# Sums by accumulating transfers of GpSimd instead of VectorE additions, in a mixed Fourier and sliding-window attention kernel

## The chip, the core and the metric

The kernel runs on one core of a Trainium2 chip. The metric is the device time of one execution in microseconds (us), the lower the better. The engines are called as the profile calls them: PE is TensorE (matmuls; PEld its weight loads), DVE is VectorE, ACT is ScalarE, POOL is GpSimd, SP is SyncE, which here only issues transfers.

## What is computed

Two layers read the same `x` (2048 rows of 512) and are mixed by a gate. All is float32.

```python
a = einsum("bsd,ed->bse", x, dft_hid_re); b = einsum("bsd,ed->bse", x, dft_hid_im)
A = einsum("ts,bse->bte", dft_seq_re, a) - einsum("ts,bse->bte", dft_seq_im, b)   # Fourier mixing

q, k, v = split(x @ wqkv)                  # 32 heads of 16
s = (q @ k.T) / 4, kept where 0 <= row - column < 256
B = (softmax(s) @ v) @ wo                  # sliding-window attention

g = sigmoid((x * gate_w).sum(-1))
out = g * A + (1 - g) * B
```

## The kernel before

**Precision.** TensorE multiplies numbers of fewer bits than float32, so every operand is kept as two tiles, a rounded "high" part (a cast, on ScalarE) and a "low" part (the original minus the high part, a 128x512 subtraction). A product is three matmuls: high by high, high by low, low by high. The low parts of the sequence-transform matrices (`lo<-raw,hi`) are made by VectorE during attention and by GpSimd once the list `FIN` is filled, when the attention loop has ended (`attention_done`).

**Two streams on TensorE.** The attention loop runs over 8 groups of 4 heads times 16 row blocks of 128 (128 steps `n`, each of four quarters). In each quarter it issues a small piece of attention and then (`fill`) a number of matmuls from `dense()`, a generator that computes everything else: projections, hidden transform, then the sequence transform. So attention is spread evenly over the dense work, and the two share the engines. All other attention work is put on an agenda by quarter (`at_time(t, ...)`), and the engines keep the order in which instructions are written out.

**Attention.** `s_pair` multiplies queries by keys into PSUM (a bank pair of the pool `ps_a`, tag `st`, two of them), and VectorE adds the mask and takes the row minimum (`junk<-s,mask` with its read-out `ml`), which frees the banks. Some steps later `t_pair` computes the transposed scores with the minimum folded in, ScalarE takes the exponential (`pt<-t`), and GpSimd zeroes what lies outside the window (`AFFINE_SELECT pt<-pt`). Every fourth step comes a *visit* (32 in all): `pv` multiplies 512 rows of `pt` by the values into two PSUM banks, one for each half of the array's rows. The visit then ends in a chain, at the offsets (in quarters) of the tuple `far`:
- `o_evict`: ScalarE copies both banks to `ots`, a tile of three 512-wide slots; the second bank always goes to slot 2, the first in turn to slot 0 or 1
- `o_add`: VectorE adds slot 2 to the other
- `l_move`: SyncE moves the softmax denominators, 4 rows of 512, to a 128x16 tile (`lt<-ots`); `l_turn`: VectorE's RECIPROCAL; `l_inv` and `l_back`: to DRAM and back, spread over the rows (`ev<-l_scr`)
- `o_mul`: GpSimd multiplies (`ev<-ots,ev`); `o_out` stores to `o_scr`.

**The sequence transform.** The output has 16 row blocks `tb`; each is a sum over 16 blocks of each of two matrix halves, cosine by `a` (half 0) and sine by `b` (half 1), in two steps `j` of eight. A step is 24 pairs of matmuls, on the upper and the lower 64 rows of the array at the same time (`halves64`). The steps are grouped in threes, and a block's steps do not all follow one another: `SWITCH`, `LATE` and the list `keys` say which come when (kind `f`: both `j` in one accumulation; kind `h`: each `j` by itself). So a partial sum, already scaled by the gate `g1`, is stored in DRAM (`r_scr`) and taken up later. The first term of a block is evicted by ScalarE and stored (`store_r`). A later term fetches the partial sum into a tile `ev` (5 buffers) 42 beats ahead (`FETCH`; a beat is one step of the dense stream), VectorE computes `ps * g1 + r` in one SCALAR_TENSOR_TENSOR (`add_to`), and SyncE stores the result in another copy of `r_scr`. There are 21 such additions. The last terms of nine blocks (`c_block`) and the output projection (`wo_...`) come after attention and are the tail.

**Loads of the sequence matrices** (`raw<-cr`, `raw<-ci`, 512 KB, three buffers) are issued by GpSimd during attention and by SyncE afterwards, each when the low parts of the piece three earlier have been made.

Of the kernel before, what the change touches and what calls it, by code (L numbers as in the profile page):

```python
# [7 lines left out]
F32 = mybir.dt.float32  # L8
F32R = mybir.dt.float32r
AF = mybir.ActivationFunctionType  # L10
OP = mybir.AluOpType
# [3 lines left out]
P = 128  # L15
# [30 lines left out]
def fnet_window_mix(ctx: ExitStack, tc: tile.TileContext, xT, x, wqk, wv, wr, wi, cr, ci, wo, gw, out):  # L46
# [15 lines left out]
    m_scr = [dram.tile([2, 16, P], F32, name=f"m_scr{i}") for i in range(32)]  # L62
    l_scr = [dram.tile([HG, 512], F32, name=f"l_scr{i}") for i in range(32)]
    o_scr = [dram.tile([NG, 32, 2, HG, 512], F32, name=f"o_scr{i}") for i in range(4)]
    r_scr = [[dram.tile([P, D], F32, name=f"r_scr{i}_{c}") for c in range(16)] for i in range(3)]

    def ld(dst, src):
        mark("sp", nc.sync.dma_start(dst, src))

    def ld_pool(dst, src):  # L70
        nc.gpsimd.dma_start(dst, src)

    def f(ap):
        return ap.bitcast(F32)
# [59 lines left out]
        return hi, lo  # L134

    jobs = []
    due = []
    beats = [0]

    def after(n, fn, *args):  # L140
        due.append((beats[0] + n, lambda: fn(*args)))  # L141
# [10 lines left out]
    def split_soon(raw, on_dve=False):  # L152
        hi = st.tile([P, 1024], F32R, name="hi")
        lo = st.tile([P, 1024], F32R, name="lo")
        for c in HALVES:
            jobs.append(lambda c=c: nc.scalar.copy(hi[:, c], raw[:, c]))  # L156
            jobs.append(lambda c=c: (nc.gpsimd if FIN else nc.vector).tensor_sub(lo[:, c], raw[:, c], f(hi[:, c])))  # L157
        return hi, lo

    def job(n):  # L160
# [305 lines left out]
        nc.scalar.copy(ots[:, 0:3:2] if i % 2 == 0 else ots[:, 1:3], o)  # L466

    def o_add(i):
        nc.vector.tensor_add(OT[i], OT[i], ots[:, 2])

    LT = {}

# [15 lines left out]
    def o_mul(i):  # L488
        ot, rl = OT.pop(i), LT.pop(i)
        nc.gpsimd.tensor_mul(rl, ot, rl)  # L490
        OT[i] = rl

    def o_out(i):
        rl = OT.pop(i)
# [155 lines left out]
    def dense():  # L650
# [138 lines left out]
        order += [ab_part(0, sb, do(*AB0.get(sb, ()))) for sb in range(16)]  # L789
        groups = [order[:4], *(order[i:i + 3] for i in range(4, len(order), 3))]  # L790

        def store_r(tb, o):
            t = ev.tile([P, 512], F32, name="ev")
            nc.scalar.activation(t, o.ps, AF.Copy, scale=g1[:, tb:tb + 1])
            after(STORE, ld, r_scr[0][tb], t)

        def fetch(src):
            def load():
                r = ev.tile([P, 512], F32, name="ev")
                ld(r, src)  # L800
                return r
            return load

        def add_to(dst, tb, o):
            nc.vector.scalar_tensor_tensor(o.r, o.ps, g1[:, tb:tb + 1], o.r, op0=OP.mult, op1=OP.add)
            after(STORE, ld, dst, o.r)

        def shortly(fn):
            return lambda o: after(2, fn, o)

        def r_in(tb):
            return r_scr[2 if tb in lasts else 0][tb]

        def finish(tb):
            return shortly(lambda o: add_to(r_scr[1][tb], tb, o))

        todo_b = [*SC]

# [6 lines left out]

        def c_get(k):
            kind, half, tb, j = k
            o = outs.get((half, tb)) if kind == "f" or j else None
            if kind == "f":
                if j == 0:  # L830
                    o = outs[half, tb] = Out(shortly(lambda o: store_r(tb, o)) if half == 0 else finish(tb), 2,
                                             None if half == 0 else fetch(r_in(tb)))
            elif half == 0:
                o = (Out(shortly(lambda o: store_r(tb, o))) if j == 0 else
                     Out(shortly(lambda o: add_to(r_scr[2][tb], tb, o)), 1, fetch(r_scr[0][tb])))
            else:
                o = (Out(shortly(lambda o: add_to(r_scr[2][tb], tb, o)), 1, fetch(r_in(tb))) if j == 0 else
                     Out(finish(tb), 1, fetch(r_scr[2][tb])))
            n = slots[kind, half, j] = slots.get((kind, half, j), -1) + 1
            mid = {4: pieces.load}  # L840
            if kind == "h" and half != j:
                if n in (1, 2, 3, 4, 5):
                    mid[12] = next_b
                if n in (1, 3, 5):
                    mid[20] = next_b
            return Part(o, lambda: c_ops(pieces.get((half, tb * 2 + j)), ab if half == 0 else nxt, j), 24,
                        pre=pieces.split, mid=mid)
# [9 lines left out]
        have.add("halves")  # L857

        def load_r(tb):
            return mixed.pop(tb, None) if tb > 13 else fetch(r_in(tb))()  # L860

        def add_r(tb, ps, r):
            nc.vector.scalar_tensor_tensor(r, ps, g1[:, tb:tb + 1], r, op0=OP.mult, op1=OP.add)
# [116 lines left out]
    def r_load(i):  # L980
        k = 4 if i == R15 else i % 2 * 2
        R[i] = RT[0][:, k], RT[0][:, k + 1]
        for tb, t in zip(O[i][0], R[i]):
            with behind("sp"):
                ld(t, r_scr[2 if i == R15 else 1][tb])

    def sums(eng, s1, s2, s3, s4, a, b):
        eng.tensor_add(s1, b[:, :256], b[:, 256:])
# [144 lines left out]
    for i in range(4 * GROUPS):  # L1133
        t = 4 * (VISIT * i + VISIT + LAG) + 3
        at_time(t + 0.5, pv, i)
        far = (0.5, 2, 3, 9, 11, 16, 21, 24) if i == 4 * GROUPS - 1 else (0.5, 2, 4, 11, 15, 21, 28, 32)
        for d, fn in zip(far, (o_evict, o_add, l_move, l_turn, l_inv, l_back, o_mul, o_out)):
            at_time(t + d, fn, i)
        if i:
            at_time(t + 2, v_next, i + 2)  # L1140
            at_time(t + 12, v_spread, i + 2)
# [75 lines left out]
```

## Time and profile before

| what | value |
|---|---|
| time, median of 2 runs | 839.9 us (839.17 to 840.64) |
| profiled execution | 838.5 us, its span 836.7 us |
| TensorE matmuls busy | 813.9 us (97%) |
| VectorE busy | 541.4 us (65%), 1536 instructions |
| ScalarE busy | 430.9 us (51%) |
| GpSimd busy | 378.6 us (45%) |
| granted TensorE clock | 0.998 of full speed |
| bytes moved by DMA | 168.98 MB, mean 202 GB/s |

The profile is one execution. Its span runs from the first to the last instruction; the execution's own time is 1.8 us longer. Lines L... are lines of the kernel file, and a line can be that of a helper: `L542` is every matmul of `halves64`, `L71` every load issued by GpSimd, `L68` every transfer issued by SyncE. In a row, `out<-in` names tiles without their numbers; `x` is the count, then busy time in us, mean ns of one, and the idle time of the engine just before with the instruction that ended it.

### The profile page before, as it was taken

The page shows a single profiled execution, that of the slowest core. Times are in us where ns is not written, and L with a number is a line of the kernel's source. Part 1 is how long each engine was busy: PE and PEld are TensorE (multiplying, and loading weights), DVE is VectorE, ACT ScalarE, POOL GpSimd, SP SyncE. Part 2 cuts the span into 40 slices and gives each one's busy share as a digit, 9 for nine tenths or more (in the row PEclk, how much of TensorE's full clock was granted, in tenths as well). Part 3 has the DMA queues.
Part 4 walks back from the last instruction along what each step waited for, and adds up shares of the span by engine and source line. Part 5 has one row for each costly group of instructions (what it writes and reads, how often), then busy time and mean ns, then how long its engine had stood idle before and what let it go on. Part 6 is the DMA issues. An engine that isn't in the chain of part 4 may idle for free.

```text
span 836.7 us, 22652 instructions
## 1 busy us (share of the span) xinstructions
PE 813.9 (97%) x8706; PEld 661.6 (79%) x8706; DVE 541.4 (65%) x1536; ACT 430.9 (51%) x814; POOL 378.6 (45%) x683
## 2 busy tenths in 40 slices
PE   9999999999999998999999999999999999899998
PEld 7899877887778777888877887777777877788886
DVE  7276765566776777666766666887887546455453
ACT  6225664556555656555655666565655653323220
POOL 5002444444444435444554444564644555765440
PEclk9999999999999999999999999999999999999999
DMA  9875887668878456555666667887885657765531
GB/s 341 288 216 154 268 264 202 182 181 293 299 256 249 114 140 180 136 176 148 189 154 185 156 182 211 233 252 229 236 230 167 198 162 226 261 196 189 168 114 51
DMA packets 109355, 168.98 MB, mean 202 GB/s; under 512 B 34240, under 2 KB 43968, under 8 KB 109248
## 3 DMA queue, kind: packets, MB, share of 16 engines
q1 hardware_dynamic: 96192, 127.04, 51.0%
q0 software_dynamic: 11088, 39.33, 15.4%
q8 instruction: 68, 1.11, 0.6%
q10 hardware_dynamic: 1968, 1.18, 0.5%
q14 instruction: 39, 0.32, 0.1%
HBM read 107.74 MB, written 59.51 MB: 200 GB/s over the span
## 4 chain that ended last, share of the span: by engine, by line
PE 77%; DVE 10%; DMA 6%; issue 4%; ACT 2%; POOL 1%; SPq 0%; DVEq 0%; POOLq 0%; ACTq 0%
PE d L542 43%; PE dc L595 8%; PE o L458 8%; PE s L364 5%; PE t L1027 5%; PE t L423 4%; DVE junk L368 4%; PE d L582 3%; DMA raw<-ci 2%; DVE lo L157 1%; DMA lt<-ots 1%; DMA o_scr<-ev 1%; DMA r_scr<-ev 1%; DVE big L141 1%; PE s L294 1%
## 5 line engine op out<-in xcount | busy, mean ns | idle before, releaser
L368 DVE CUSTOM_DVE_ANT_0 junk<-s,mask 128x384 f32<-128x384 f32 (+2 forms) x512 | 272.0, 531 | 174.4 <-PE s L364 163.6
L542 PE MATMUL d<-big,hi 64*128 64x512 f32 x1920 | 345.7, 396 | 0.0
L428 POOL TENSOR_SCALAR_AFFINE_SELECT pt<-pt 128x256 f32<-128x256 f32 x256 | 122.3, 478 | 340.1 <-ACT pt L426 274.7
L426 ACT ACTIVATE pt<-t 128x768 f32<-128x768 f32 (+2 forms) x256 | 197.8, 773 | 113.3 <-PE t L423 109.6
L542 PEld LDWEIGHTS d<-big,hi 64*128 64x128 f32 x1920 | 192.3, 186 | 24.5 <-issue 0.9
L542 PE MATMUL d<-big,lo 64*128 64x512 f32 x960 | 205.4, 395 | 0.0
L542 PE MATMUL d<-hi,big 64*128 64x512 f32 x672 | 135.7, 395 | 0.0
L542 PEld LDWEIGHTS d<-big,lo 64*128 64x128 f32 x960 | 98.9, 186 | 12.4 <-issue 0.5
L364 PE MATMUL s<-ring,ring 48*128 48x384 f32 (+2 forms) x512 | 96.3, 342 | 6.7 <-DVE ml L368 6.2
L156 ACT CAST hi<-raw 128x512 fp32r<-128x512 f32 x142 | 87.1, 618 | 25.9 <-DMA raw<-ci 15.4
L432 POOL TENSOR_SCALAR_AFFINE_SELECT pt<-pt 128x256 f32<-128x256 f32 x224 | 94.6, 422 | 0.0
L595 PE MATMUL dc<-big,hi 128*128 128x512 f32 x284 | 92.1, 394 | 0.0
L157 DVE TENSOR_TENSOR lo<-raw,hi 128x512 fp32r<-128x512 f32 x110 | 85.5, 779 | 9.6 <-ACT hi L156 9.6
L423 PE MATMUL t<-ring,ring 50*128 50x384 f32 (+2 forms) x512 | 87.2, 328 | 0.8 <-DMA ring<-m_scr 0.3
L542 PEld LDWEIGHTS d<-hi,big 64*128 64x128 f32 x672 | 78.9, 186 | 6.6 <-issue 0.2
L542 PE MATMUL d<-lo,big 64*128 64x512 f32 x336 | 84.0, 394 | 0.0
L364 PEld LDWEIGHTS s<-ring,ring 48*128 48x128 f32 x512 | 53.5, 184 | 37.4 <-DVE ml L368 23.4
L458 PEld LDWEIGHTS o<-pt,vt 64*32 64x32 f32 x2816 | 53.9, 106 | 28.9 <-issue 9.2
L458 PE MATMUL o<-pt,vt 64*32 64x320 f32 (+4 forms) x2816 | 74.7, 348 | 2.1 <-DVE ml L368 1.9
L466 ACT COPY ots<-o 128x1024 f32<-128x1024 f32 x32 | 32.5, 1016 | 73.6 <-PE o L458 31.0
L157 POOL TENSOR_TENSOR lo<-raw,hi 128x512 fp32r<-128x512 f32 x32 | 43.8, 1379 | 39.6 <-ACT hi L156 39.5
L423 PEld LDWEIGHTS t<-ring,ring 50*128 50x128 f32 x512 | 50.3, 184 | 12.8 <-ACT pt L426 1.3
(124 smaller groups left out, 914.6 us busy)
## 6 DMA issues: line engine op xcount, KB each, us to landing
ring<-qk_scr SPq DMA_DIRECT2D x128, 192.0 KB
qk_scr<-home SPq DMA_DIRECT2D x32, 512.0 KB
raw<-cr POOLq DMA_DIRECT2D x32, 512.0 KB, 5.2
r_scr<-ev SPq DMA_DIRECT2D x44, 256.0 KB
raw<-ci POOLq DMA_DIRECT2D x18, 512.0 KB, 6.3
qk_scr<-home SPq DMA_DIRECT2D x32, 256.0 KB
ev<-l_scr SPq DMA_DIRECT2D x32, 256.0 KB
o_scr<-ev SPq DMA_DIRECT2D x32, 256.0 KB
```

Of the source, the lines that this page charges most:

```text
L156: jobs.append(lambda c=c: nc.scalar.copy(hi[:, c], raw[:, c]))
L157: jobs.append(lambda c=c: (nc.gpsimd if FIN else nc.vector).tensor_sub(lo[:, c], raw[:, c], f(hi[:, c])))
L364: nc.tensor.matmul(ps[:, h, :w], ring[0][r, p, j * P:j * P + P], ring[1][r, p, k0:k0 + w], start=True, stop=True)
L368: mark("dve", nc.vector.tensor_tensor_reduce(out=junk[:, :w], in0=ps[:, h, :w], in1=mask[:, WIN - w:], scale=1.0, scalar=3e38, op0=OP.add, ...
L423: nc.tensor.matmul(ps[:, h, :w], ring[1][r, p, q0:q0 + P], ring[0][r, p, q0:q0 + w], start=True, stop=True)
L426: nc.scalar.activation(pt[:, ph, :w], ps[:, :, :w], AF.Exp, scale=-1.0)
L428: nc.gpsimd.affine_select(a, a, pattern=[[0, 2], [1, P]], compare_op=OP.is_ge, fill=0.0, base=0, channel_multiplier=-1)
L432: nc.gpsimd.affine_select(a, a, pattern=[[0, 2], [-1, P]], compare_op=OP.is_gt, fill=0.0, base=0, channel_multiplier=1)
L458: nc.tensor.matmul(o[32 * j:32 * j + 32, h, a - q0:e - q0], v[r, kb % 4, 32 * j:32 * j + 32], PT[G * NB + kb][r, j, a - kb * P:e - kb * P] ...
L542: nc.tensor.matmul(o.ps, lhs[r], rhs[r], start=start, stop=end and o.left == 0, skip_group_check=True)
L595: nc.tensor.matmul(ps, w[a][:, i % 8 * 128:i % 8 * 128 + 128], ab[SC[i]][:, b], start=i == ends[0] and a + b == 0, stop=i == ends[1] and a ...
L1027: nc.tensor.matmul(ps, o[:, a, c], fin(n, b, c), start=start and c == 0 and a + b == 0, stop=c == 1 and a == 1, skip_group_check=True)
```

## The change

- **A visit's two banks.** `o_add` no longer is a VectorE instruction but a transfer issued by GpSimd, from slot 2 of `ots` into slot 0 or 1 with the option that adds to the target. `l_move` comes one quarter later (offset 5 instead of 4); in the last visit the offsets from `l_move` on are 1 or 1.5 later.
- **Partial sums.** Every term is evicted by ScalarE with the gate's factor. The first of a block is stored by SyncE as before, each later one is added to the block in DRAM by an accumulating transfer of GpSimd. The fetches, VectorE's additions and the third copy of `r_scr` are gone. The last terms of nine blocks (`c_block`) still fetch and add on VectorE.
- **Low parts.** GpSimd takes over the low parts when the last visit's `o_mul` has been written out, not at the end of the attention loop; seven of them so stay on VectorE.

TensorE's instructions and their order are the same.

```diff
+    def add_pool(dst, src):
+        nc.gpsimd.dma_start(dst, src, accum_op=OP.add)
...
     def split_soon(raw, on_dve=False):
...
-            jobs.append(lambda c=c: (nc.gpsimd if FIN else nc.vector).tensor_sub(lo[:, c], raw[:, c], f(hi[:, c])))
+            jobs.append(lambda c=c: (nc.gpsimd if done else nc.vector).tensor_sub(lo[:, c], raw[:, c], f(hi[:, c])))
...
     def o_add(i):
-        nc.vector.tensor_add(OT[i], OT[i], ots[:, 2])
+        add_pool(OT[i], ots[:, 2])
...
     def o_mul(i):
...
+        if i == 4 * GROUPS - 1:
+            done.append(True)
...
+        sent = set()
+
         def store_r(tb, o):
             t = ev.tile([P, 512], F32, name="ev")
             nc.scalar.activation(t, o.ps, AF.Copy, scale=g1[:, tb:tb + 1])
-            after(STORE, ld, r_scr[0][tb], t)
+            after(STORE, add_pool if tb in sent else ld, r_scr[0][tb], t)
+            sent.add(tb)
...
-        def add_to(dst, tb, o):
-            nc.vector.scalar_tensor_tensor(o.r, o.ps, g1[:, tb:tb + 1], o.r, op0=OP.mult, op1=OP.add)
-            after(STORE, ld, dst, o.r)
...
         def c_get(k):
             kind, half, tb, j = k
...
-            elif half == 0:
-                o = (Out(shortly(lambda o: store_r(tb, o))) if j == 0 else
-                     Out(shortly(lambda o: add_to(r_scr[2][tb], tb, o)), 1, fetch(r_scr[0][tb])))
-            else:
-                o = (Out(shortly(lambda o: add_to(r_scr[2][tb], tb, o)), 1, fetch(r_in(tb))) if j == 0 else
-                     Out(finish(tb), 1, fetch(r_scr[2][tb])))
+            o = outs.get((half, tb)) if kind == "f" and j else None
+            if o is None:
+                o = outs[half, tb] = Out(shortly(lambda o: store_r(tb, o)), 2 if kind == "f" else 1)
...
-        far = (0.5, 2, 3, 9, 11, 16, 21, 24) if i == 4 * GROUPS - 1 else (0.5, 2, 4, 11, 15, 21, 28, 32)
+        far = (0.5, 2, 4.5, 10, 12, 17, 22, 25) if i == 4 * GROUPS - 1 else (0.5, 2, 5, 11, 15, 21, 28, 32)
         for d, fn in zip(far, (o_evict, o_add, l_move, l_turn, l_inv, l_back, o_mul, o_out)):
```

Three places show what moves. First VectorE at the visit that the profile has at 558.7 us, in the stage of second terms. ISA rows are the mask-and-reduce pairs, `big<-stage` and `lo<-raw,hi` are low parts. Before:

```order
L141 TENSOR_TENSOR big<-stage,big 128x512
L368 ISA junk,ml<-s,mask 128x384
L368 ISA ml 128x1
L368 ISA junk,ml<-s,mask 128x384
L368 ISA ml 128x1
L469 TENSOR_TENSOR ots<-ots 128x512
L805 SCALAR_TENSOR_TENSOR ev<-d,g_309,ev 128x512
L157 TENSOR_TENSOR lo<-raw,hi 128x512
L368 ISA junk,ml<-s,mask 128x384
```

And with the change, at the same place on VectorE:

```order
L145 TENSOR_TENSOR big<-stage,big 128x512
L372 ISA junk,ml<-s,mask 128x384
L372 ISA ml 128x1
L372 ISA junk,ml<-s,mask 128x384
L372 ISA ml 128x1
L161 TENSOR_TENSOR lo<-raw,hi 128x512
L372 ISA junk,ml<-s,mask 128x384
```

The visit's addition and the addition of a partial sum are gone from between the reductions and the next low part.

Second, GpSimd at the same visit. `AFFINE_SELECT` rows are the window masks on `pt`, `stage` and `raw` are loads. Before:

```order
L71 DMA stage<-ab_scr_11_129 128x512
L71 DMA raw<-ci 128x1024
L428 AFFINE_SELECT pt<-pt 128x2x128
L432 AFFINE_SELECT pt<-pt 128x2x128
L428 AFFINE_SELECT pt<-pt 128x2x128
L432 AFFINE_SELECT pt<-pt 128x2x128
L428 AFFINE_SELECT pt<-pt 128x2x128
L432 AFFINE_SELECT pt<-pt 128x2x128
```

And with the change, on GpSimd:

```order
L71 DMA stage<-ab_scr_11_129 128x512
L71 DMA raw<-ci 128x1024
L432 AFFINE_SELECT pt<-pt 128x2x128
L436 AFFINE_SELECT pt<-pt 128x2x128
L74 DMA ots<-ots 128x512
L432 AFFINE_SELECT pt<-pt 128x2x128
L436 AFFINE_SELECT pt<-pt 128x2x128
L74 DMA r_scr_13_215<-ev 128x512
```

The accumulating transfers of the visit and of a partial sum now stand between the masks, behind the mask of the first exponential after the visit's eviction.

Third, SyncE at the same visit, from the load of the values to the next ring load. Before:

```order
L68 DMA vr<-v_scr_112 128x4x64
L68 DMA lt<-ots 128x1x16
L68 DMA ev<-l_scr_189 128x1x512
L68 DMA r_scr_13_247<-ev 128x512
L68 DMA r_scr_15_249<-ev 128x512
L68 DMA ev<-r_scr_0_202 128x512
L68 DMA r_scr_14_248<-ev 128x512
L68 DMA ring_285<-qk_scr_3_1_91 48x2x512
```

And with the change, on SyncE:

```order
L68 DMA vr<-v_scr_112 128x4x64
L68 DMA ev<-l_scr_189 128x1x512
L68 DMA lt<-ots 128x1x16
L68 DMA ring_269<-qk_scr_3_1_91 48x2x512
L68 DMA ring_270<-qk_scr_3_1_107 48x2x512
```

The move of the denominators has gone behind the visit before's `ev<-l_scr`, and the stores and fetches of partial sums behind it are gone.

More of the change, by code (lines that the diff above doesn't have):

```diff
@@ L64, in fnet_window_mix @@
     o_scr = [dram.tile([NG, 32, 2, HG, 512], F32, name=f"o_scr{i}") for i in range(4)]
-    r_scr = [[dram.tile([P, D], F32, name=f"r_scr{i}_{c}") for c in range(16)] for i in range(3)]
+    r_scr = [[dram.tile([P, D], F32, name=f"r_scr{i}_{c}") for c in range(16)] for i in range(2)]
     def ld(dst, src):
@@ L136, in fnet_window_mix @@
     jobs = []
+    done = []
     due = []
@@ L802, in fetch @@
             return load
-        def add_to(dst, tb, o):
-            nc.vector.scalar_tensor_tensor(o.r, o.ps, g1[:, tb:tb + 1], o.r, op0=OP.mult, op1=OP.add)
-            after(STORE, ld, dst, o.r)
         def shortly(fn):
             return lambda o: after(2, fn, o)
[L811 to L815, printed above, removed]
         todo_b = [*SC]
@@ L827, in c_get @@
             kind, half, tb, j = k
[L828 to L832, printed above, removed]
-            elif half == 0:
-                o = (Out(shortly(lambda o: store_r(tb, o))) if j == 0 else
-                     Out(shortly(lambda o: add_to(r_scr[2][tb], tb, o)), 1, fetch(r_scr[0][tb])))
-            else:
-                o = (Out(shortly(lambda o: add_to(r_scr[2][tb], tb, o)), 1, fetch(r_in(tb))) if j == 0 else
-                     Out(finish(tb), 1, fetch(r_scr[2][tb])))
+            o = outs.get((half, tb)) if kind == "f" and j else None
+            if o is None:
+                o = outs[half, tb] = Out(shortly(lambda o: store_r(tb, o)), 2 if kind == "f" else 1)
             n = slots[kind, half, j] = slots.get((kind, half, j), -1) + 1
@@ L859, in load_r @@
         def load_r(tb):
-            return mixed.pop(tb, None) if tb > 13 else fetch(r_in(tb))()
+            return mixed.pop(tb, None) if tb > 13 else fetch(r_scr[0][tb])()
         def add_r(tb, ps, r):
@@ L984, in r_load @@
             with behind("sp"):
-                ld(t, r_scr[2 if i == R15 else 1][tb])
+                ld(t, r_scr[int(i != R15 and tb >= 16 - LATE)][tb])
     def sums(eng, s1, s2, s3, s4, a, b):
```

## The prediction

> **What bounds the kernel now.** I read the page's first lines, then the same busy times by stage, then what TensorE waited for.
>
> ```profile
> span 836.7 us, 22652 instructions
> PE 813.9 (97%) x8706; PEld 661.6 (79%) x8706; DVE 541.4 (65%) x1536; ACT 430.9 (51%) x814; POOL 378.6 (45%) x683
> ```
>
> TensorE (PE) is busy for all but 22.8 us of the span, and the change leaves its instructions and their order alone. So whatever is won has to come out of those 22.8 us, and any loss is a new wait of TensorE.
>
> ```profile
> core 0: us, PE busy (x) PEld busy (x) DVE busy (x) ACT busy (x) POOL busy (x), PEclk, DMA share, GB/s
> 100.00:340.00 240.00, 232.00 (x2858) 184.46 (x2856) 162.44 (x524) 137.34 (x264) 107.31 (x223) 1.00 0.71 214
> 340.00:520.00 180.00, 179.64 (x2296) 145.17 (x2294) 120.49 (x382) 107.66 (x195) 84.37 (x175) 1.00 0.64 172
> 520.00:640.00 120.00, 115.08 (x1389) 89.47 (x1395) 96.70 (x276) 69.31 (x126) 64.83 (x124) 1.00 0.79 229
> 640.00:700.00 60.00, 60.00 (x700) 47.88 (x683) 34.51 (x66) 33.27 (x62) 28.59 (x53) 1.00 0.63 187
> 700.00:836.00 136.00, 128.89 (x710) 108.32 (x708) 63.70 (x106) 33.29 (x68) 67.75 (x62) 0.99 0.52 169
> ```
>
> Column one is the stage, two its length, three TensorE's busy time. TensorE idles 8.0 us in 100 to 340 (projections and the hidden transform), 0.4 in 340 to 520 (first terms of the sequence transform), 4.9 in 520 to 640 (where second terms are added to partial sums), nothing in 640 to 700, 7.1 in the tail. Who is waited for:
>
> ```profile
> PE s L364 <- DVE ml L368: 6.2, 13, 0.9
> PE s L384 <- DVE ml L368: 3.7, 7, 1.0
> PE o L458 <- DVE ml L368: 1.9, 3, 1.4
> PE t L1027 <- ACT ex L141: 3.8, 1, 3.8
> ```
>
> Columns: total, times, longest. 11.8 us in 23 waits go to VectorE (DVE), whose mask-and-reduce pair (L368) frees the PSUM bank that TensorE needs next. One wait of 3.8 lies in the tail. One of the 23, in the stage that the change lightens most:
>
> ```profile
> 560.71 0.69 DVE L469 TENSOR_TENSOR ots<-ots 128x512 f32<-128x512 f32 x1
> 561.32 0.75 DVE L805 SCALAR_TENSOR_TENSOR ev<-d,g,ev 128x512 f32<-128x512 f32 x1
> 561.98 0.77 DVE L157 TENSOR_TENSOR lo<-raw,hi 128x512 fp32r<-128x512 f32 x1
> 562.66 0.55 DVE L368 CUSTOM_DVE_ANT_0 junk<-s,mask 128x384 f32<-128x384 f32 x1
> 563.87 0.44 PE L364 MATMUL s<-ring,ring 48*128 48x384 f32 x2 [0.73 <-DVE ml L368]
> ```
>
> Three 128x512 instructions stand ahead of the reductions, and TensorE waits 0.73 us. The first two are exactly the two kinds that the change removes.
>
> **The change part by part.** The prices:
>
> ```profile
> L469 DVE TENSOR_TENSOR ots<-ots 128x512 f32<-128x512 f32 x32 | 22.0, 686 | 4.8 <-ACT ots L466 4.8
> L805 DVE SCALAR_TENSOR_TENSOR ev<-d,g,ev 128x512 f32<-128x512 f32 x21 | 15.5, 739 | 12.4 <-PE d L542 12.4
> L794 ACT ACTIVATE ev<-d,g 128x512 f32<-128x512 f32 x16 | 11.0, 688 | 0.6 <-PE d L542 0.6
> L157 DVE TENSOR_TENSOR lo<-raw,hi 128x512 fp32r<-128x512 f32 x110 | 85.5, 779 | 9.6 <-ACT hi L156 9.6
> L157 POOL TENSOR_TENSOR lo<-raw,hi 128x512 fp32r<-128x512 f32 x32 | 43.8, 1379 | 39.6 <-ACT hi L156 39.5
> L71 POOL DMA_DIRECT2D raw<-cr x32 | 18.1, 567 | 0.8 <-issue 0.8
> 520.00:640.00 120.00, 10.29 (x14) 1.00 0.79 229
> ```
>
> The last row counts VectorE's instructions on `ev` in 520 to 640: 14 of the 21 partial-sum additions, 10.3 us.
>
> *VectorE, 520 to 640.* Gone are these 14 and six visit additions (6 x 0.686 = 4.1), together 14.4 of 96.7 us. What stays, 82.3 in 120 us, is 69% busy; the stage 340 to 520 runs at 120.5/180 = 67% with 0.4 us of idle TensorE. I take the same for this stage, about 0.5 instead of 4.9: **-4.4** (bounds -4.9 and 0, the latter if the waits only move).
>
> *VectorE, 100 to 340.* Here 12 additions go (8.2 us of 162.4). The stage is already at 68%, so density is not what hurts; single pile-ups are. Of its 13 waits of TensorE that carry VectorE's name, from the first to the last
>
> ```profile
> 114.83 0.44 PE L364 MATMUL s<-ring,ring 48*128 48x384 f32 x2 [0.26 <-DVE ml L368]
> 334.56 0.44 PE L364 MATMUL s<-ring,ring 48*128 48x384 f32 x2 [0.45 <-DVE ml L368]
> ```
>
> five have a visit addition in the VectorE work just ahead (3.0 us together), and an addition can give back no more than its 0.69: **-2.8** (bounds -3.0 and 0). The others sit behind low parts and gate products, which stay.
>
> *ScalarE.* It evicts the 21 second terms instead: 21 x 0.688 = 14.4 us, 14 of them in 520 to 640, where it goes from 69.3 to 78.9 us of 120 (66%). The cover is the spare bank of the `t` products; the one row of a wait there is small:
>
> ```profile
> PEld t L423 <- ACT pt L426: 1.3, 3, 0.5
> PEld o L458 <- POOL pt L432: 4.3, 6, 1.8
> ```
>
> **+0.5** (bounds 0 and 4.4, what the same instructions cost on VectorE). In exchange these evictions wait for no fetched partial sum.
>
> *GpSimd (POOL).* 32 + 21 = 53 issues more at the price of a load's, 0.567: 30.1 us. Seven low parts leave (7 x 1.38 = 9.7), so it ends near 399 us, 48%. Behind each issue stand the mask selects of `pt`, which a visit's products need four steps later; six times TensorE's weight loads already wait there. Each issue can push one of those by 0.57, 3.4 in all; I take **+0.5** (bounds 0 and 3.4). Here the Trainium skill speaks against the change: in "SBUF — State Buffer", section "SBUF: two separate sides", it warns that DMAs issued from GpSimd starve while VectorE runs an instruction that takes both shared ports, since GpSimd cannot write their descriptors. By that rule I would take the upper bound, 3.4. The trace does not show it: the 32 issues above mean 0.567 us next to a VectorE that is two thirds busy, so I keep 0.5.
>
> *The new wait.* SyncE's move of the denominators (`lt<-ots`) now waits for the accumulating transfer, and VectorE's reciprocal (L478) keeps its place. The visit of the example above, the tightest visit outside the end, and the nearest durations:
>
> ```profile
> 562.15 0.85 POOL L432 TENSOR_SCALAR_AFFINE_SELECT pt<-pt 128x256 f32<-128x256 f32 x1
> 571.93 0.25 DVE L478 RECIPROCAL lt<-lt 128x16 f32<-128x16 f32 x1
> 169.26 0.40 POOL L432 TENSOR_SCALAR_AFFINE_SELECT pt<-pt 128x256 f32<-128x256 f32 x1
> 177.10 0.25 DVE L478 RECIPROCAL lt<-lt 128x16 f32<-128x16 f32 x1
> DMA to landing us min/median/max: 2.9/5.8/8.1
> 690.05 0.56 SPq L68 DMA_DIRECT2D lt<-ots  x1
> 695.48 0.25 DVE L478 RECIPROCAL lt<-lt 128x16 f32<-128x16 f32 x1 [0.55 <-DMA lt<-ots]
> DVE junk L368 <- PE s L364: 163.6, 137, 7.1
> ```
>
> GpSimd can issue the addition after the select, at 563.0, and the reciprocal stood at 571.9: 8.9 us of room (7.4 in the tight visit). No accumulating transfer is in the trace. The nearest is a load of the same 256 KB on the same queue: the row of 2.9/5.8/8.1 is that of the 20 `stage<-ab_scr` loads. The small move behind it took 5.4 in the crowded tail (690.05 to 695.48) and, as the fastest transfer of that row, hardly under 2.9. So the chain is 5.8 at best from two times 2.9, 13.5 at worst, and I take 5.8 + 3.0 = 8.8, the median load and a move near its fast end, since outside the tail no reciprocal waited. That fits the room of an ordinary visit by a hair and misses the tight one by 1.4 us. VectorE itself waits 163.6/137 = 1.2 us for TensorE at a typical pair, which absorbs most of it. Behind a late reciprocal stand the next reductions and low parts, and TensorE behind those. I take **+2** (bounds 0 and 32, below). The skill's fit in "DMA: Bandwidth & Descriptors", section "Anatomy of one DMA — SWDGE (gpsimd) path", of 2.0 us plus bytes over 436 GB/s is an estimate of 2.6 us for 256 KB, with which this +2 would be 0; the loads here took 5.8, and I go by them.
>
> *SyncE* loses 42 transfers (21 stores, 21 fetches) and gains a block of some 7 us per visit at `lt<-ots`; behind it stand ring loads that the old trace issued no earlier than at 572 in this visit, so I cost it at nothing. Without that cover a late ring load would stop TensorE, up to the size of the late chain itself.
>
> *The tail.* The 3.8 us wait is a chain:
>
> ```profile
> 700.71 2.55 POOL L157 TENSOR_TENSOR lo<-raw,hi 128x512 fp32r<-128x512 f32 x2 [0.45 <-ACT hi L156]
> 703.29 0.35 SPq L68 DMA_DIRECT2D raw<-ci  x1
> 713.18 0.62 ACT L156 CAST hi<-raw 128x512 fp32r<-128x512 f32 x1 [5.43 <-DMA raw<-ci]
> ```
>
> GpSimd's two low parts end at 703.26 and free the buffer, the next load goes out, lands 9.8 us later, and ScalarE is stuck behind it. On VectorE the two take 2 x 0.78, 1.0 us less. Against that, the last visit's `lt<-ots` (690.05) waits for its accumulation: eviction ended at 685.8, an issue of 0.6 and 5.8 of landing make 692.2, and the first of these loads stands behind it on SyncE. So 2 us later there, 1 earlier here: **+0.5** (bounds -5, if wait and the slow products after it vanish, and +6, if each of three reciprocals holds the low parts by 2).
>
> **Sum:** -4.4 - 2.8 + 0.5 + 0.5 + 2 + 0.5 = -3.7. The profiled execution took 838.5 (span plus 1.8), so 834.8; the median of the two timed runs, 839.9, lies 1.4 above it: **836**.
>
> **The rivals.**
> 1. *Slower: the reciprocal waits in every visit.* If the transfer takes 5.8 and the move 5.4, the chain is 11.2, 2.3 over the room and 1.1 over room plus slack. 29 visits before the tail then cost 32 us instead of 2: **866**. It decides from a chain of 8.9 + 1.2 = 10.1 us on. For it: that an accumulation must also read its target. Against: the fast end of the rows.
> 2. *More is won.* VectorE's relief takes away all waits of 100 to 640 but those of the quiet density, 12.9 us, and the new wait costs nothing: 838.5 - 12.9 + 1.4 = **827**. Against: eight of 13 waits in 100 to 340 have no removed instruction ahead.
> 3. *No change.* Evictions on ScalarE and issues on GpSimd delay `pt` as much as VectorE is relieved, so the change of engine buys nothing: 838.5 - 3.7 + 4.4 + 0.5 + 1.4 = **841**.
>
> **How the numbers follow.** The forecast, 831 to 842 by its smaller bounds, gets 0.50, rival 1 0.17, rival 2 0.13, rival 3 0.20. The range 825 to 862 holds the forecast, rivals 2 and 3, and the milder half of rival 1 (a chain near 10.5). Within 2% (about what a measurement of this kernel tells from no change) is 823.1 to 856.7: 0.83; slower 0.13, most of rival 1; faster 0.04, beyond rival 2.
>
> **What would show it.** In the new profile: VectorE near 510 us; TensorE idle under 1 us in the stage of second terms; reciprocals waiting for `lt<-ots` in few visits outside the end; accumulating rows on GpSimd of about 0.57 us landing near 6. I am wrong if reciprocals wait in most visits, if `t` products start to wait for ScalarE, or if the issue rows on GpSimd are several times as long.

## The result: 891.4 us, six per cent slower, and the profile after

The changed kernel takes 891.44 us (median of 2 runs, 888.26 to 894.63) against 839.9: a ratio of 1.061, 95% interval 1.045 to 1.078. The forecast was 836, range 825 to 862. Rival 1, the reciprocal that waits for the denominators, is what happened, in 19 visits and at a higher price than its 866.

The page's first lines, of the profiled execution after:

```profile
span 892.9 us, 22556 instructions
PE 828.5 (93%) x8706; PEld 670.4 (75%) x8706; DVE 513.2 (57%) x1490; ACT 442.2 (50%) x835; POOL 407.9 (46%) x729
```

VectorE is relieved as planned (513 us for 541), and it didn't help. The span is 56.2 us longer. TensorE idles 64.4 us (892.9 less 828.5) instead of 22.8, and the same 8706 matmuls are busy for 14.6 us longer. By stage (columns as in the prediction; the boundaries lie where TensorE reaches the work it had reached at 340, 520, 640 and 700):

```profile
100.00:363.00 263.00, 238.14 (x2860) 187.92 (x2858) 156.78 (x516) 137.48 (x265) 114.61 (x235) 0.97 0.73 208
363.00:546.00 183.00, 180.01 (x2292) 145.44 (x2290) 115.03 (x369) 107.58 (x195) 91.35 (x184) 0.99 0.68 180
546.00:680.00 134.00, 119.62 (x1380) 93.07 (x1384) 85.72 (x256) 76.68 (x138) 80.21 (x144) 0.95 0.78 188
680.00:750.00 70.00, 62.25 (x705) 48.74 (x689) 21.55 (x53) 37.09 (x69) 33.57 (x59) 0.93 0.61 144
750.00:893.00 143.00, 130.71 (x715) 109.64 (x713) 70.21 (x117) 33.30 (x68) 62.64 (x59) 0.98 0.52 167
```

The stages are 23, 3, 14, 10 and 6 us longer than before. The least is lost in the stage of first terms. Who waits (total, times, longest), of the list of waits:

```profile
DVE lt L482 <- DMA lt<-ots: 65.2, 19, 10.5
PE s L368 <- DVE ml L372: 27.0, 14, 8.5
PE o L462 <- POOL pt L432: 6.0, 1, 6.0
PE t L1018 <- ACT ex L145: 5.9, 1, 5.9
SPq L68 <- DMA ots<-ots: 283.4, 31, 13.3
```

The reciprocal (L482) waited 4.1 us in 3 visits before, now 65.2 in 19 of 32, and TensorE's wait for the reductions behind it grew from 6.2 to 27.0. The last row is new: SyncE stands still in 31 visits, 9.1 us on average, until the accumulation has landed. Not all of that is lost: SyncE waited 125.1 us for `t` products before and waits 37.7 for them now.

One quiet visit, from the timelines of GpSimd, SyncE, VectorE and TensorE (start, length, engine; in brackets the wait just before):

```profile
490.59 0.90 POOL L74 DMA_DIRECT2D ots<-ots  x1
498.58 0.56 SPq L68 DMA_DIRECT2D lt<-ots  x1
500.46 0.25 DVE L482 RECIPROCAL lt<-lt 128x16 f32<-128x16 f32 x1 [1.07 <-DMA lt<-ots]
502.45 0.44 PE L368 MATMUL s<-ring,ring 48*128 48x384 f32 x2 [0.68 <-DVE ml L372]
```

8.0 us from issue to the denominators' move, 1.9 for the move: a chain of 9.9 us, and VectorE is 1.07 us late. And the worst one, visit 8:

```profile
260.57 0.89 POOL L74 DMA_DIRECT2D ots<-ots  x1
271.00 1.17 SPq L68 DMA_DIRECT2D lt<-ots  x1
279.54 0.25 DVE L482 RECIPROCAL lt<-lt 128x16 f32<-128x16 f32 x1 [10.51 <-DMA lt<-ots]
282.20 0.58 PE L368 MATMUL s<-ring,ring 48*128 48x256 f32 x2 [8.47 <-DVE ml L372]
```

with the windows around TensorE's new start (columns as in the stages above, the granted clock third from the end)

```profile
276.00:278.00 2.00, 0.00 (x0) 0.00 (x0) 0.00 (x0) 0.00 (x0) 0.00 (x0) 0.69 0.85 273
282.00:284.00 2.00, 1.80 (x10) 1.51 (x12) 1.29 (x7) 0.00 (x0) 0.00 (x0) 0.50 0.32 82
286.00:288.00 2.00, 2.00 (x50) 1.01 (x56) 0.00 (x0) 0.00 (x0) 0.63 (x2) 0.75 0.32 87
288.00:290.00 2.00, 2.00 (x66) 1.73 (x52) 0.00 (x0) 0.95 (x2) 0.00 (x0) 1.00 0.87 269
```

Here the chain takes 19 us: 10.4 until the move is issued, and then 8.5 for its 8 KB, behind stores that SyncE had issued ahead of it. VectorE stands for 10.5 us, TensorE for 8.5, and when TensorE starts again its granted clock is 0.50 for some five microseconds (282.2 to 287). The accumulation itself had landed 9.1 us after its issue; SyncE, busy with stores and a load, came to the move 1.3 us later, and the trace's packets of the move run only from 276.6 to 279.1. The 14.6 us of slower matmuls go with that second bill: over the whole execution the clock is 0.971 of full speed, and it was 0.998. As an estimate, twice the missing share of the span, that is 52 us at half clock against 3.

How far the end of each visit's eviction has fallen behind that of the kernel before, as differences of the two timelines, shows where the time goes: most visits lose under a microsecond, while 2.1 us are lost between visits 2 and 3, 7.0 between 6 and 7, 12.6 between 8 and 9, 3.6 between 14 and 15, 7.8 between 22 and 25, 8.5 between 26 and 27, 8.7 between 29 and 31, and 7.3 from visit 31 to the end. Nearly each follows a reciprocal that waited over 2 us (one of 4.9 us, in visit 28, was followed by no loss); waits below that cost at most 1.0, as VectorE's own slack of 1.2 us lets one expect.

### The profile page after: what moved, and what is told of

The parts are those of the page before. It is cut to its first block, busy times and chain, and to the rows that moved or that the text cites. A ratio compares the mean times of both kernels' runs of the same rounds, so it can differ in the third digit from the quotient of the medians.

```text
span 892.9 us, 22556 instructions
## 1 busy us (share of the span) xinstructions
PE 828.5 (93%) x8706; PEld 670.4 (75%) x8706; DVE 513.2 (57%) x1490; ACT 442.2 (50%) x835; POOL 407.9 (46%) x729
## 4 chain that ended last, share of the span: by engine, by line
PE 65%; DMA 17%; DVE 7%; issue 5%; POOL 2%; ACT 2%; SPq 1%; DVEq 0%; ACTq 0%; POOLq 0%
PE d L548 35%; PE dc L601 7%; PE o L462 7%; DMA lt<-ots 5%; PE t L1018 4%; DMA ots<-ots 4%; PE s L368 4%; PE t L427 3%; DVE junk L372 3%; PE d L588 2%; DMA ev<-l_scr 2%; DMA raw<-ci 2%; DMA stage<-ab_scr 1%; ACT pt L430 1%; SPq L68 1%
## 5 line engine op out<-in xcount | busy, mean ns | idle before, releaser
L548 PE MATMUL d<-big,hi 64*128 64x512 f32 x1920 | 350.7, 400 | 3.2 <-DVE home L113 3.2
L432 POOL TENSOR_SCALAR_AFFINE_SELECT pt<-pt 128x256 f32<-128x256 f32 x256 | 124.4, 488 | 328.5 <-ACT pt L430 265.8
L548 PEld LDWEIGHTS d<-big,hi 64*128 64x128 f32 x1920 | 195.4, 189 | 28.1 <-DVE home L113 3.6
L548 PE MATMUL d<-big,lo 64*128 64x512 f32 x960 | 207.8, 400 | 0.0
L161 DVE TENSOR_TENSOR lo<-raw,hi 128x512 fp32r<-128x512 f32 x117 | 89.3, 764 | 21.7 <-ACT hi L160 16.3
L436 POOL TENSOR_SCALAR_AFFINE_SELECT pt<-pt 128x256 f32<-128x256 f32 x224 | 100.5, 449 | 0.0
L462 PE MATMUL o<-pt,vt 64*32 64x320 f32 (+4 forms) x2816 | 79.6, 364 | 8.0 <-POOL pt L432 6.0
L601 PEld LDWEIGHTS dc<-big,hi 128*128 128x128 f32 x284 | 53.4, 192 | 9.4 <-issue 0.7
```

What stands on the lines that cost most here:

```text
L161: jobs.append(lambda c=c: (nc.gpsimd if done else nc.vector).tensor_sub(lo[:, c], raw[:, c], f(hi[:, c])))
L432: nc.gpsimd.affine_select(a, a, pattern=[[0, 2], [1, P]], compare_op=OP.is_ge, fill=0.0, base=0, channel_multiplier=-1)
L436: nc.gpsimd.affine_select(a, a, pattern=[[0, 2], [-1, P]], compare_op=OP.is_gt, fill=0.0, base=0, channel_multiplier=1)
L462: nc.tensor.matmul(o[32 * j:32 * j + 32, h, a - q0:e - q0], v[r, kb % 4, 32 * j:32 * j + 32], PT[G * NB + kb][r, j, a - kb * P:e - kb * P] ...
L548: nc.tensor.matmul(o.ps, lhs[r], rhs[r], start=start, stop=end and o.left == 0, skip_group_check=True)
L601: nc.tensor.matmul(ps, w[a][:, i % 8 * 128:i % 8 * 128 + 128], ab[SC[i]][:, b], start=i == ends[0] and a + b == 0, stop=i == ends[1] and a ...
```

## The experiments

Their medians are compared with the kernel before, run beside them on the same chip (839.6 to 840.6 us). Differences to the changed kernel rest on its two runs, 888.3 and 894.6 us, and are good to some 5 us at best; "reciprocal waits" are the row `DVE lt <- DMA lt<-ots` of each list of waits.

**1 to 3: the three parts apart.** `e1_visits`: the kernel before with

```diff
     def o_add(i):
-        nc.vector.tensor_add(OT[i], OT[i], ots[:, 2])
+        add_pool(OT[i], ots[:, 2])
-        far = (0.5, 2, 3, 9, 11, 16, 21, 24) if i == 4 * GROUPS - 1 else (0.5, 2, 4, 11, 15, 21, 28, 32)
+        far = (0.5, 2, 4.5, 10, 12, 17, 22, 25) if i == 4 * GROUPS - 1 else (0.5, 2, 5, 11, 15, 21, 28, 32)
```

> Only the visit addition goes to the accumulating transfer (with the change's new offsets of the visit); partial sums and low parts stay as before. Theory A (the reciprocal waits for the denominators, VectorE stands still with it, the reductions behind it come late, TensorE idles and then runs at half clock): nearly the whole loss is here, 880 to 895 us, reciprocal waits of 50 to 70 us in all as in the changed kernel (65.2). Rival B (GpSimd's 53 accumulating issues and their traffic cost by their number, wherever they stand): 32 of 53 are here, so about 60% of the loss, 865 to 875.

Measured: 882.6 us, ratio 1.049 (1.046 to 1.053), reciprocal waits 49.8 us in 17 visits, just under theory A's 50. `e2_sums` is the changed kernel with these lines and the low parts put back:

> Only the partial sums of the sequence transform are accumulated by transfers; visit addition, its offsets and the low parts as before. Theory A: nobody on VectorE waits for these transfers, so 832 to 841 us, with reciprocal waits of under 6 us as before (4.1) and fewer than 10 waits of TensorE for VectorE in the stage of second terms. Rival B: 21 of 53 issues, about 40% of the loss, 855 to 865.

Measured: 838.7 us, ratio 0.998 (0.996 to 1.000). `e3_low` is the kernel before with

```diff
-            jobs.append(lambda c=c: (nc.gpsimd if FIN else nc.vector).tensor_sub(lo[:, c], raw[:, c], f(hi[:, c])))
+            jobs.append(lambda c=c: (nc.gpsimd if done else nc.vector).tensor_sub(lo[:, c], raw[:, c], f(hi[:, c])))
```

and the line that fills `done`.

> Only the last low parts stay on VectorE until the last visit is multiplied; additions and sums as before. Theory A and rival B alike: 835 to 842 us, since VectorE has room there (34.5 of 60 us busy in 640 to 700) and the 3.8 us wait in the tail may go. A rival C (low parts on VectorE delay the tail's reductions) gives 845 to 855.

Measured: 841.3 us, ratio 1.001 (1.000 to 1.002). So the loss comes with the visits (+42.5 us), and the sums and low parts by themselves are worth 1 us each way. With all three it is 8.8 us more than with the visits alone, but the intervals of the two ratios overlap, so whether the parts add up isn't shown. The 21 issues of the sums by themselves cost nothing, which speaks against rival B.

**4 to 6: where is the loss within a visit?** Three versions of the changed kernel differ in the offsets of an ordinary visit:

```diff
-(0.5, 2, 5, 11, 15, 21, 28, 32)
+(0.5, 2, 5, 14, 18, 24, 31, 35)     # e4_room
+(0.5, 2, 5, 14, 17, 20.5, 28, 32)   # e5_turn
+(0.5, 2, 9, 14, 17, 21, 28, 32)     # e6_free
```

> The changed kernel with the reciprocal and all that follows it in an ordinary visit three quarter steps (some 3.8 us) later: 14, 18, 24, 31, 35 in place of 11, 15, 21, 28, 32; the last visit as in the change. Theory A: the chain then has some 12.7 us in place of 8.9, most of the 65 us of reciprocal waits go (under 15 left), and the time falls to 838 to 855. Rival B: the same transfers are made, so 880 to 895. Rival D (SyncE, stopped some 9 us in each visit at the move of the denominators, delays the ring loads and stores behind it): SyncE is still stopped, 865 to 890, with reciprocals that no longer wait.

> The changed kernel with only the reciprocal (14 for 11), the store of its result (17 for 15) and the load back (20.5 for 21) moved in an ordinary visit; the multiply and the store out stay at 28 and 32, so that the load back no longer stands behind SyncE's stop in the next visit, as it did where all five were moved. Theory A (the reciprocal's wait is the loss): 836 to 848 us, under 15 us of reciprocal waits outside the tail, and the multiply on GpSimd waits no more than before. Theory D (the loss comes from SyncE, stopped at the move of the denominators for some 9 us a visit, and from what it issues late): SyncE is still stopped, 855 to 870.

> As the run before, but the move of the denominators also later (9 for 5), so that SyncE reaches it when the accumulation has nearly landed; reciprocal at 14, store 17, load back 21, multiply 28, store out 32. Theory A: the same as the run before within 4 us. Theory D: 10 us or more below it, 835 to 848, with SyncE's waits for the accumulation falling from 283 us to under 100.

Measured: 865.3 (ratio 1.032, 1.026 to 1.037), 871.9 (1.038, 1.035 to 1.041) and 872.6 (1.041, 1.037 to 1.046). The waits of the first two:

```profile
DVE lt L482 <- DMA lt<-ots: 17.1, 5, 7.6
POOL ev L494 <- DMA ev<-l_scr: 59.1, 19, 13.3
ACT ots L470 <- POOL ev L494: 58.1, 17, 10.4
```
```profile
DVE lt L482 <- DMA lt<-ots: 35.8, 8, 9.1
SPq L68 <- DMA ots<-ots: 91.8, 30, 7.6
SPq L68 <- DMA l_scr<-lt: 155.2, 29, 9.7
```

Room for the reciprocal gives back 26 and 20 us, where theory A expected at least 36 and 43. The same transfers at 865 us speak against rival B (880 to 895), while rival D's ranges are met in `e4_room` (865 to 890) and missed by 2 us in `e5_turn` (855 to 870). In `e4_room` the reciprocal's wait is nearly gone (17.1 us in 5 visits), but the load back stands on SyncE behind the next visit's stop, GpSimd's multiply waits 59 us for it, and the eviction that needs its slot 58: the same lateness in another place. In `e5_turn` visits 9 to 22 lose nothing (they gain 2.9 us), and what remains is 6 us after visit 6, 6 after visit 26, and 19 from visit 29 on. After visit 6 no reciprocal had waited; the list of waits from 222 to 232 us has

```profile
ACT home L107 <- DMA qk_scr<-home: 4.9, 1, 4.9
PE t L427 <- ACT pt L430: 3.7, 1, 3.7
```

ScalarE waits for stores that SyncE issues, and TensorE for ScalarE: a second path, which is rival D's and not the reciprocal's. `e6_free` comes within 1 us of `e5_turn`, as theory A has it, but tells nothing about SyncE: its stops for the accumulation were to fall from 283 us, but in `e5_turn` they are 92 already (SyncE stands at the load back instead), and 94 here.

**7: a wait without an accumulation.** `e7_wait` is `e2_sums` with the move issued at the reciprocal's place, `(0.5, 2, 11, 11, 15, 21, 28, 32)`.

> The price of the reciprocal's wait by itself: partial sums accumulated by transfers, but the visit addition on VectorE, and the move of the denominators issued only at the reciprocal's own place (11 for 4). The reciprocal then waits for a small transfer in every visit, some 2 us, and SyncE is stopped by nothing. Theory A: VectorE's slack of 1.2 us a visit takes half of it, so 0.8 us in 29 visits and some more where TensorE drops to half clock, 855 to 875 us, against 838.7 without the edit. Theory D: 836 to 842.

Measured: 864.6, ratio 1.030 (1.026 to 1.035), and

```profile
DVE lt L482 <- DMA lt<-ots: 38.5, 14, 7.3
```

With the addition on VectorE and no accumulation that SyncE waits for, late denominators cost 26 us over `e2_sums`. SyncE's waits are 555 us in all, for 551 there, so its stops hardly differ. This is the cleanest evidence for theory A. The wait was not 2 us in every visit but 14 waits of up to 7.3.

**8: is it the accumulation?** `e8_copy`: the changed kernel with

```diff
-        nc.scalar.copy(ots[:, 0:3:2] if i % 2 == 0 else ots[:, 1:3], o)
+        nc.scalar.copy(ots[:, 0:3:2] if i % 2 == 0 else ots[:, 1:3], o[:, 0:1].broadcast_to([P, 2, 512]))
-        add_pool(OT[i], ots[:, 2])
+        ld_pool(OT[i], ots[:, 2])
```

> The changed kernel with a plain transfer of the same 256 KB in place of the accumulating one of the visit (the eviction puts the first bank into both places; the second bank's part is left out of the result). Theory E (the accumulation is what makes the transfer slow, by reading its target): it lands in under 5.8 us, the issue takes 0.57 us, reciprocal waits fall below 25 us, 845 to 865 us. Theory F (any such transfer of GpSimd takes this long between these stages): landing near 6.8 as with the accumulation, 60 us of waits, 883 to 897.

Measured: 871.5, ratio 1.037 (1.033 to 1.041). Issue and landing of these transfers in the changed kernel and in this one (minimum, median, maximum, in ns and us):

```profile
L74 POOL DMA_DIRECT2D ots<-ots x32: 857/902/929, 92.4 to 735.0; - x32
DMA to landing us min/median/max: 3.3/6.8/9.5
```
```profile
L71 POOL DMA_DIRECT2D ots<-ots x32: 553/567/586, 92.4 to 707.0; - x32
DMA to landing us min/median/max: 2.3/5.8/9.7
```

Between E and F: adding costs 0.34 us in the issue, and the time is 20 us lower without it. That it costs 1.0 us in the landing isn't shown: the median landing of the same accumulation is anything from 5.1 to 7.3 us in the versions that make it in 26 visits or more. A plain copy of the same size at the same place still loses 32 us; its reciprocals wait 38.1 us.

**9 and 10: few visits or all?** The changed kernel with a choice in `o_add`: `e9_others` accumulates where `i not in (6, 8, 26, 29, 30, 31)`, `e10_six` where `i in` that list; the rest adds on VectorE.

> The changed kernel with the visit addition back on VectorE in six of 32 visits (6, 8, 26, 29, 30, 31: those after which the ends of the evictions had fallen back most against the kernel before, 44 of the 56 us together with the end); all offsets as in the change. Theory G (the loss sits in a few visits where the chain of accumulation and move meets full DMA queues or the tail): 845 to 855 us. Rival H (the chain is over its room in every visit, and each pays its share of some 1.6 us): 875 to 885.

> The other way round: only these six visits accumulate by a transfer, 26 add on VectorE; offsets, partial sums and low parts as in the change. Theory G: most of the loss is back, 870 to 888 us. Rival H: six shares, 845 to 853.

Measured: 869.4 (1.035, 1.033 to 1.036) and 867.7 (1.032, 1.029 to 1.035). The two losses are 29.1 and 27.4 us, and theory G and rival H are both wrong by themselves: six visits hold about half, 26 the other half. (Both have the change's offsets, so their sum of 56.5 counts the price of these, experiment 13, twice.) In `e9_others` visit 8 loses 8.3 us although it adds on VectorE. That the change had moved something else there is the next question.

**11 and 12: parts that keep out of the way.** `e11_quiet` is `e2_sums` with accumulation in the visits 9 to 21 only, at the offsets of `e5_turn`; `e12_tail` is `e5_turn` with visits 28 to 31 on VectorE at the offsets of before.

> Partial sums accumulated by transfers, and the visit addition only in the visits 9 to 21, with the reciprocal's place moved there as in the run with 14, 17, 20.5; the other visits and the low parts as before the change. In these visits that run gained 2.9 us on the kernel before. Theory G: 834.5 to 838.5 us, 1 to 4 us under the run with the partial sums alone (838.7). Rival H: 845 to 860.

> The run with the reciprocal at 14 (871.9 us), but the last four visits (28 to 31) add on VectorE at the offsets of before. That run loses 19 of its 31 us from visit 29 on. Theory G (the tail is a place of its own: three visits close together at the end, with the last loads behind them on SyncE): 852 to 858 us. Rival (the tail is late only because of what came before, and pays anyway): 866 to 873.

Measured: 836.6 us, ratio 0.996 (0.994 to 0.998), the first version with accumulation in visits that isn't slower, 3.7 us under the kernel before and not clearly under `e2_sums` (0.996 to 1.000); and 864.1 (1.028, 1.025 to 1.030), where 852 to 858 was expected. The tail by itself gives 8 us back, no more: in the profiled run visit 8 loses 7.7 us in place of 1.7, and 5.8 are lost after visit 22. Both versions are written alike up to visit 27, so what one visit loses can differ by 6 us from execution to execution, and a reading of single visits, each from one profile, is no better than that.

**13: the offsets alone.** `e13_offsets` is the kernel before with only the two lines of `far` from experiment 1. On SyncE, the order of instructions in before (-) and in it (+) in an ordinary visit:

```diff
-L68 DMA lt<-ots 128x1x16
 L68 DMA ev<-l_scr_166 128x1x512
+L68 DMA lt<-ots 128x1x16
```

> The kernel before with nothing but the change's offsets: the move of the denominators one quarter step later (5 for 4), on SyncE behind the load back of the visit before; additions stay on VectorE. Theory I (the new place costs by itself, where the queue behind that load is full, as after visit 8): 848 to 858 us, reciprocal waits of 15 to 30 us. Theory J (the place alone costs nothing, only the wait for the accumulation): 838 to 843, reciprocal waits under 8 us.

Measured: 851.5, ratio 1.014 (1.011 to 1.017), reciprocal waits 14.7 us in 6 visits: theory I, whose waits were to be 15 at least. Visit 8 in before, and here:

```profile
251.62 0.60 SPq L68 DMA_DIRECT2D lt<-ots  x1
252.32 1.15 SPq L68 DMA_DIRECT2D qk_scr<-home  x2
253.52 0.85 SPq L68 DMA_DIRECT2D ev<-l_scr  x1
257.37 0.25 DVE L478 RECIPROCAL lt<-lt 128x16 f32<-128x16 f32 x1
```
```profile
252.59 0.96 SPq L68 DMA_DIRECT2D qk_scr<-home  x2
253.60 0.95 SPq L68 DMA_DIRECT2D ev<-l_scr  x1
254.60 1.18 SPq L68 DMA_DIRECT2D lt<-ots  x1
262.13 0.25 DVE L478 RECIPROCAL lt<-lt 128x16 f32<-128x16 f32 x1 [2.98 <-DMA lt<-ots]
264.74 0.39 PE L364 MATMUL s<-ring,ring 48*128 48x256 f32 x2 [2.70 <-DVE ml L368]
```

One quarter step puts 8 KB behind a load and, here, two large stores. The reciprocal has them 7.5 us after the issue, and waits; before, 5.8 us after it, they were there. Visits 9 to 22 lose nothing, and in the tail the reciprocals of visits 29 and 30 wait 4.8 and 5.8 us. So the 11 us are those of a few visits, and the last visit's new offsets are among what was changed.

**14: SyncE's stop alone.** `e14_block` is `e2_sums` with a copy by GpSimd and a small transfer of SyncE that waits for it, and that nobody needs:

```diff
+    def b_copy(i):
+        ld_pool(blk[i], ots[:, 2])
+
+    def b_move(i):
+        ld(blk2[i], blk[i][:, :16])
...
+        at_time(t + 2, b_copy, i)
+        at_time(t + (4.5 if i == 4 * GROUPS - 1 else 5), b_move, i)
```

> SyncE's stop by itself: partial sums accumulated, visit addition and denominators as before the change, but in every visit GpSimd also copies the second bank (256 KB) to a scratch in DRAM that nobody needs, and SyncE issues a small transfer that waits for it, at the place where the changed kernel moves the denominators. Theory D (SyncE's stop delays stores and ring loads): 850 to 870 us, with VectorE hardly waiting for denominators (under 12 us) and TensorE idle behind ScalarE, which waits for stores. Theory A: 838 to 844, the price of the extra traffic at most.

Measured: 848.6, ratio 1.011 (1.008 to 1.014), just under D's 850 and above A's 844; reciprocal waits 11.4 us.

```profile
SPq L68 <- DMA blk<-ots: 118.0, 31, 9.2
```
```profile
224.19 0.60 ACT L107 ACTIVATE home<-d 128x512 fp32r<-128x512 f32 x1 [3.50 <-DMA qk_scr<-home]
226.06 0.44 PE L427 MATMUL t<-ring,ring 50*128 50x384 f32 x2 [1.87 <-ACT pt L430]
```

The stop does cost, though the profiled execution, 854.9 us, was the slowest of the four: SyncE issues the stores of `home` late, ScalarE waits 3.5 us for a free buffer, and TensorE 1.9 for the exponentials behind it. These stops are 118 us in all, though (first row, of the waits; the others are of the timelines), the changed kernel's 283, and the copies add traffic, so the 10 us are neither an upper nor a lower bound of SyncE's share there.

**15 and 16.** `e15_early` is the changed kernel with the addition issued at 1, not at 2; `e16_nineteen` is `e11_quiet` with the visits 9 to 19.

> The changed kernel with the addition's issue one quarter step (1.27 us) earlier on GpSimd, ahead of one pair of mask selects (1 for 2); all else as in the change. Theory A with a chain that is over its room by about a microsecond in most visits: each of the 19 waits gets up to 1.2 us shorter, 870 to 880 us, reciprocal waits near 45 instead of 65 us. Theory G (a few visits with full queues, which 1.2 us can't help): 883 to 891.

> As the run with quiet visits (836.6 us), but the addition accumulated only in the visits 9 to 19, since after visits 20 and 21 that run lost 1.6 us to a reciprocal wait of 2.7. Theory G: 833.5 to 837.5 us. If the waits are where the traffic of the day falls and not in those visits, 836 to 839.

Measured: 882.7 (1.049, 1.046 to 1.053) with reciprocal waits of 46.0 us, and 838.2 (0.997, 0.996 to 0.999). The earlier issue takes 19 us off the waits as theory A says, but only some 9 off the time, within the spread of the changed kernel: visit 8 still loses 10.8. The last misses its 833.5 to 837.5, lies within the other reading's 836 to 839, and doesn't differ from `e11_quiet` by more than their intervals; visits 20 and 21 made no difference, and what both gain on before is 0.1 to 0.6 per cent.

## Why the prediction was wrong, step by step

- **The new wait: +2 taken, 42.5 measured (experiment 1), 11 of it by the offsets alone (next point).** This is the step that failed. The typical values were right: a median landing of 6.8 us for 5.8, a move of 1.9 in a quiet stage for 3.0, in sum 8.7 against 8.8. Wrong was to price the wait at them. The move is issued 3.4 to 10.4 us after the accumulation's issue and, where the reciprocal waited, takes 1.9 to 8.5 more; with a room equal to the typical chain, half of the visits must be late, the early ones give nothing back, and 19 of 32 were. The bounds given for the chain, 5.8 to 13.5, were passed in four visits (13.7 to 19.0). And the reason for a move near its fast end, that outside the tail no reciprocal waited, did not carry: in the trace before, the reciprocal stood 5.4 to 10.8 us behind the move's issue (median 9.4), so that moves of several microseconds stayed hidden. Rival 1's 32 us for the wait lie close to 42.5 less 11, but by luck: it took 29 waits alike of 1.1 us, and there were 19, of 0.2 to 10.5.
- **The move keeps its price: failed.** The change puts it one quarter step later, behind the load back of the visit before, and its new offsets by themselves cost 11 us (experiment 13). The prediction named the offset and priced only the reciprocal's room, not the queue that the move was moved past.
- **SyncE's stop at nothing: failed.** It named ring loads as what stands behind, and they were not the ones that were late first. The stores of `home` were (experiment 14, about 10 us for a shorter stop, and visit 6 of `e5_turn`). How much of the changed kernel's loss is SyncE's stays open.
- **A wait costs what it lasts: failed in the worse visits.** After TensorE's longer waits the clock halves (0.50 after the 8.5 us of visit 8), and 14.6 of the 56.2 us are matmuls that took longer. Rival 1's 32 us had no term for it.
- **VectorE's relief: about right where it falls, but not kept.** In the second-term stage `e2_sums` idles 2.2 us (117.00 less 114.78 in the row below) in place of 4.9. That is 2.7 of the predicted 4.4 without the visits' share, and TensorE's waits for VectorE there are 3 of 1.5 us in all, for 10 of 4.5. `e11_quiet` gains 2.0 us on before between visits 8 and 14; the prediction had 2.8 for the stage from 100 to 340.

```profile
521.00:638.00 117.00, 114.78 (x1398) 90.06 (x1402) 90.10 (x262) 76.83 (x140) 75.98 (x138) 1.00 0.83 202
714.11 1.65 PE L1018 MATMUL t<-fin,ring 128*128 128x256 f32 x6 [6.03 <-ACT ex L145]
```

  The sum takes this gain as time. In the profiled execution of `e2_sums`, 3.6 us are gained between visits 22 and 29 and 3.8 lost again from there to the end, and its median is only 1.4 us under the kernel before. The second row shows where: the tail's one long wait, 3.8 us before, is 6.0 here and ends at the same 714.1 us. What TensorE wins ahead of it, it waits there.

- **ScalarE's 21 evictions, +0.5: fits.** The sums alone are 1.4 us faster in the median, so nothing large is hidden there.
- **GpSimd's issues at 0.567: mis-sized.** The two groups below (count, busy us, mean ns) cost 49 us of GpSimd, not 30, and the page shows 408 us busy for the 399 foretold. By themselves the 21 of the sums cost nothing that the time shows.

```profile
L74 POOL DMA_DIRECT2D ots<-ots x32 | 28.9, 903 | 2.5 <-issue 1.4 <-ACT ots L470 1.1
L74 POOL DMA_DIRECT2D r_scr<-ev x21 | 20.3, 967 | 6.8 <-issue 6.7
```

- **The tail, +0.5 within -5 and +6: failed**, 16 us from visit 29 to the end. The chain there is again the reciprocal's:

```profile
728.70 0.25 DVE L482 RECIPROCAL lt<-lt 128x16 f32<-128x16 f32 x1 [9.33 <-DMA lt<-ots]
729.41 0.75 DVE L916 TENSOR_TENSOR spare<-tw 128x256 f32<-128x256 f32 x2
729.86 0.58 POOL L71 DMA_DIRECT2D raw<-ci  x1 [8.13 <-DVE spare L916]
731.02 2.38 PE L462 MATMUL o<-pt,vt 64*32 64x256 f32 x60 [6.00 <-POOL pt L432]
```

VectorE stands 9.3 us, differences of blocks of `wo` (`spare`) stand behind it, GpSimd's next load waits 8.1 us for them, the mask selects wait behind that load, and TensorE 6.0 for the selects. Four engines in program order pass one late transfer on. The low parts kept on VectorE were no gain (+1 us, within 0 to 2).

Its own list of signs did work: reciprocals that wait in most visits were named as what would make it wrong. That late denominators cost time, through VectorE, is shown (experiments 4, 7 and 13); what stays open is the exact split of the 51 us between them and SyncE's late stores. Taking away half of the accumulating visits, or the tail, or 3.8 us of lateness each gives 8 to 26 us, and these overlap.

## What to carry to other kernels

A wait on an engine that works in program order is priced by the distribution of what it waits for against the room, not by its median: room has to cover the slow transfers, and early ones earn nothing. A transfer in place of an instruction was free here only where nobody in program order needed its result soon: the partial sums, which nobody waits for, could go (0.998), the visits only where the queues were quiet (0.996 with the sums). Time that TensorE wins ahead of a wait for something else, as in the tail, can be waited away there. And when a step is moved by one place, list what it now stands behind on its queue: the new offsets, which put 8 KB behind a load and at times a few stores, cost 11 us.

## What the runs showed of the hardware that was not expected

- A transfer of 8 KB took 1.9 us from issue in a quiet visit (19) and 8.5 behind large ones (visit 8).
- An accumulating transfer within SBUF of 256 KB took 0.90 us to issue, a plain one of the same shape 0.57. The landing, 6.8 us in the median and 3.3 to 9.5 in the changed kernel, is not told apart from the plain one's 5.8 (2.3 to 9.7): in other versions the accumulation's median was as low as 5.1.
- The clock dropped to half after waits of only 2 us:

```profile
556.00:560.00 4.00, 1.92 (x18) 1.31 (x18) 0.92 (x4) 1.86 (x5) 1.59 (x4) 1.00 0.65 162
560.00:564.00 4.00, 4.00 (x24) 2.87 (x22) 3.39 (x9) 2.66 (x5) 2.64 (x4) 0.57 0.98 219
```

TensorE idled 2.08 us of the first window and had a granted clock of 0.57 in the second; after a wait of 2.11 us at 145 it kept 1.00. The trace's record of the clock tells the two apart: it changes at 228.97, 235.80, 276.76, 287.00, 406.46, 409.88, 560.06 and 563.48, among others, always whole multiples of 3.41 us apart. Of the 3.41 us that ended at 560.06 TensorE had idled 1.9; the wait at 145 has 1.5 us in the stretch that ends at 147.05 and the rest in the one before. In this trace every stretch at full clock with 1.9 us of idle time or more lowered it, and none with 1.7 or less did; in the other runs those with 1.4 to 1.9 went either way. The Trainium skill, "TensorE: Matmul & The Clock Gate", section "What's actually happening", has the clock at half after an idle window of about 3.4 us, in windows that run free of the program, and back at full after one as long that is busy. The two levels, the window's length and its running free agree with this trace; the window needn't be idle throughout, though, since 1.9 us of its 3.41 were enough at 560.
